# Local attention and a three-layer product: maxima one group ahead, a low part moved, one value product moved

## Chip, cores and metric

The kernel runs on one core of a Trainium2 chip. The metric is device time in microseconds of one execution, the median of the runs shown. TensorE (PE, with its weight loads as PEld), VectorE (DVE), ScalarE (ACT), GpSimd (POOL) and SyncE (SP) each work through a queue of their own, and wait for one another by semaphores.

## The reference

Four batches of eight heads, 768 positions, head size 64. A query sees the 96 keys up to itself and the first 8 keys, with a bias that falls with distance; after the softmax and the product with the values the heads are put together to 3072 rows of 512, which go through four matrices in fp32:

```python
scores = scale * np.matmul(q, k.transpose(0, 1, 3, 2)) + bias
scores = np.where(keep, scores, -1000000000.0)
a = np.exp(scores - np.max(scores, axis=-1, keepdims=True))
a = a / (np.sum(a, axis=-1, keepdims=True) + 1e-09)
x = np.matmul(a, v)            # then heads side by side: 3072 x 512
out = ((x @ w1) * (x @ w2)) @ w3 @ w_out
```

## The kernel before

**Attention.** Queries are cut into 24 blocks s of 128, and the blocks into 12 pairs d = s // 2. A block has four query groups q of 32. `scores` (line 684 on) makes all scores of a block on PE: for an even block the groups 0 and 1 go into two buffers of the shared PSUM pool (tile `more`), the rest into columns 104 to 511 of the tile `sc`. `maxima(s, q)` is two DVE instructions (line 709) that add the bias, take the row maximum and write the result to `pr`; `exponentials(s, q)` is two ACT instructions (line 716) on the same rows. `sums`, `scale_part` and `turn` (lines 721, 738, 746) are DVE's: reciprocal of the sums, scaling, and a transpose into `pt`. `values(d)` (line 760) multiplies a pair's transposed rows with the values on PE into columns 0 to 255 of `sc`, and `tokens(d)` (line 786) copies that on ACT into SBUF. So the scores of the next pair that lie in `sc` need that copy to be done.

**The products.** Two pairs make a unit of 512 rows. For unit 1 the first layer is done in 32 slices `U` of six 512-column matmuls (`first`, lines 278 to 280): per block f two slices, a gate copy on ACT (line 285), two slices, a product on DVE (line 288), a high part on ACT (line 293) and a low part on DVE (line 298). Beside that DVE and ACT build sums of weight blocks (`join`, `combine`, `sums_high`, `sums_low`, lines 200 to 213), which SP stores to DRAM and brings back (lines 218, 238). Units 2 to 5 do the same layer with seven half-size products (`Sevenths`, slices `P` of six 256-column matmuls, line 372), which gather in two PSUM tiles x and y and are taken out by ACT and DVE (lines 386 to 395); high and low part are lines 401 and 406. The last two products are folded into one: 32 slices `Z` of three 512-column matmuls (`third`, lines 310 to 312), eight for each of four row tiles t; the eighth of a tile needs the high and low part of the last block of the line. The tiles o, x, y, m and more share four PSUM buffers in turn.

**Order.** Up to unit 1 the order of all queues is written out by hand (`ORDER`). From there `planned` makes a list of slices, each with the work of ACT and DVE that follows it; entries marked 1 are issued after the matmuls of the next slice. `rounds(d, every, parts)` goes through a pair's two blocks and lets `on(k)` issue the next k slices in between; `go(place[...])` issues all slices up to a named one. On PE, ACT and DVE the instructions stand in the order written; SP's order is made by the framework's planner. A round of an odd pair begins with the last two `P` slices of its unit and goes on through `Z`; a round of an even pair from 6 on begins at slice 0 of tile t = 3 of the unit before, where `Z` and the first `P` slices of the next unit alternate, and where `first_tokens` and `next_tokens` (lines 81, 82, 795, 798) turn the copied tokens into high and low parts of the seven blocks.

Of the kernel before, what the change touches and what calls it, by code (L numbers as in the profile page):

```python
# [20 lines left out]
P = 128  # L21
# [10 lines left out]
NR = P // R  # L32
# [376 lines left out]
def line(u):  # L409

    return list(range(NFC)) if u % 2 == 0 or u < 2 else list(range(NFC))[::-1]
# [164 lines left out]
def banded(ctx, tc, ff, ns, nt, n1, nf, oki, qk, vx, sc, pr):  # L576
# [96 lines left out]
    def frame(s, q):  # L673

        return (0 if s % NB else WIN - R * q), KF

    def scored(s, u, q, w0, w1):

        if s < PAIRS:
            k = FR + q % 2 * KF  # L680
            return sc[:, 2 * u + q // 2, k + w0:k + w1]
        if s % 2 == 0 and q < 2:
            return more[s // 2][u][:, q * KF + w0:q * KF + w1]
        i, j = (q - 2, 0) if s % 2 == 0 else (q // 2, 1 + q % 2)
        k = F3 + j * KF
        return sc[:, 2 * u + i, k + w0:k + w1]
# [15 lines left out]
    def maxima(s, q):  # L702

        if q == 0:
            stats[s] = [at.tile([P, NR, 2], F32, tag=t, bufs=2, name=f"{t}_{s}") for t in ("mx", "sm")]
        w0, w1 = frame(s, q)
        for u in range(2):
            bias = (biasw if s % NB else bias0)[:, u, q, w0:w1]
            nc.vector.tensor_tensor_reduce(out=pr[:, q, u, GLB + w0:GLB + w1], in0=scored(s, u, q, w0, w1), in1=bias, scale=-SCALE, scalar=3.0e38, op0=ALU.add, op1=ALU.min, accum_out=stats[s][0][:, q, u:u + 1])  # L709
# [148 lines left out]
    def planned():  # L858

        def of(u, name):  # L860
            return lambda *x: getattr(units[u], name)(*x)

        last = NC // 2 - 1
        pieces = [(ff.sums_high, 2), (ff.sums_low, 2)]
        for k in range(3, NFC):
            pieces += [(ff.join, k), (ff.combine, k), (ff.sums_high, k), (ff.sums_low, k)]
        for f in range(NFC):
            for m in range(2):
                for half in range(2):
                    todo = [(0, of(1, "first"), f, m, half)]  # L870
                    if half:
                        todo += [(0, of(1, "gate"), f)] if m == 0 else [(0, of(1, "product"), f), (0, of(1, "high"), f), (1, of(1, "low"), f)]
                    elif f > 1:
                        todo += [(0, ff.blocks_out, f)] if m == 0 else []
                    if m == 0 or f > 3:
                        for _ in range(2 if m == half == 0 and f > 0 else 1):
                            if pieces and not (m and half):
                                call, k = pieces.pop(0)
                                todo.append((0, call, k))
                                if call == ff.sums_low:  # L880
                                    todo.append((0, ff.sums_out, k))
                    if (f, m, half) in ((5, 0, 0), (7, 1, 1)):
                        todo += [(0, ff.bring, k, g) for k in ((0, 2) if f == 5 else (1, 3)) for g in range(3)]
                    yield [("U", 1, f, m, half)] + todo
        assert not pieces

        def seventh(u, j, p):
            unit = of(u, "multiply"), of(u, "take")
            f = line(u)[j]
            todo = [(0, unit[0], p, f), (0 if p in (1, 5, 6, 7, 4) else 1, unit[1], p, f)]  # L890
            if p == 1 and j > 1:
                todo += [(0, of(u, "high"), line(u)[j - 2]), (1, of(u, "low"), line(u)[j - 2])]
            return [("P", u, j, p)] + todo

        for u in range(1, last + 1):
            if u > 1:
                for j in range(1, NFC):
                    for p in (1, 5, 4, 6, 2, 3, 7):
                        yield seventh(u, j - 1 if p in (4, 3) else j, p)
            tail = [seventh(u, NFC - 1, p) for p in (4, 3)] if u > 1 else []  # L900
            if tail:
                f = line(u)[-2]
                tail[0] += [(0, of(u, "high"), f), (1, of(u, "low"), f)]
            if u < last:
                yield from tail
                tail = []
            for t in range(2 * T // P):
                for j, f in enumerate(line(u)):
                    todo = [(0, of(u, "third"), t, f, line(u)[0], line(u)[-1])]
                    if j == NFC - 1:  # L910
                        todo.append((0, of(u, "store"), t))
                    if t == 0 and j == 3 and u > 1:
                        todo += [(0, of(u, "high"), line(u)[-1]), (0, of(u, "low"), line(u)[-1])]
                    if u < last and (t, j) == (1, 0):
                        todo.append((0, first_tokens, u + 1))
                    if u < last and (t, j) in ((2, 5), (2, 6), (3, 0), (3, 1), (3, 2), (3, 3)):
                        todo.append((0, next_tokens, u + 1))
                    yield [("Z", u, t, j)] + todo
                    if t == 0 and j in (1, 2) and tail:
                        yield tail.pop(0)  # L920
                    if t == 3 and j < 5 and u < last:
                        yield seventh(u + 1, 0, (1, 5, 6, 2, 7)[j])

    with tc.manual_schedule(engines={mybir.EngineType.PE}):
        with tc.manual_schedule(engines={mybir.EngineType.DVE, mybir.EngineType.SP, mybir.EngineType.Activation, mybir.EngineType.Pool}):
            ordered()
        with tc.manual_schedule(engines={mybir.EngineType.Activation, mybir.EngineType.DVE}):
            plan = list(planned())
            place = {x[0]: i for i, x in enumerate(plan)}
            done = [0]  # L930

            waiting = []

            def go(until):
                for _, *todo in plan[done[0]:until]:
                    (_, call, *x), *rest = todo
                    call(*x)
                    for call, x in waiting:
                        call(*x)
                    waiting.clear()  # L940
                    for late, call, *x in rest:
                        if late:
                            waiting.append((call, x))
                        else:
                            call(*x)
                done[0] = max(done[0], until)

            def on(k):
                go(done[0] + k)

            def rounds(d, every, parts):
                for s in (2 * d, 2 * d + 1):
                    for q in range(NR):
                        maxima(s, q)
                        exponentials(s, q)
                        on(every)
                    if parts > 1:
                        on(2)
                    sums(s)
                    cuts = [(k * NR // parts, (k + 1) * NR // parts) for k in range(parts)]  # L960
                    for step in (scale_part, turn):
                        for q0, q1 in cuts:
                            step(s, q0, q1)
                            if parts > 1:
                                on(1)
                    if parts == 1 and s % 2 == 0:
                        on(5)

            scores(STEPS)
            scores(STEPS + 1)  # L970
            for d in range(STEPS // 2, n // 2):
                u = d // 2 - 1
                load(d)
                ahead = [s for s in (2 * d + 2, 2 * d + 3) if s < n]
                for s in ahead:
                    keys(s)
                rounds(d, *((1, 1) if d % 2 else (1, 2) if u == 1 else (3, 2)))
                go(place["Z", u, 2, 5] if d % 2 else place["U", u, 5, 1, 0] if u == 1 else place["P", u, 5, 5])
                values(d)
                tokens(d)  # L980
                if ahead:
                    go(place["Z", u, 3, 0] if d % 2 else place["Z", u, 0, 0] if u == 1 else place["P", u, 7, 4])
                for s in ahead:
                    scores(s)
            ok = nc.values_load(oki[0:1, 0:1])
            tc.mark_branch_hint_location("rest", engines=(mybir.EngineType.SP, mybir.EngineType.Activation))
            go(len(plan))
# [40 lines left out]
```

## Time and profile before

| | |
|---|---|
| runs | 539.74, 538.71, 537.92 us; median 538.71 |
| profiled execution | 538.34 us, span 536.5 us |
| PE | 512.3 us busy (95%), 6148 matmuls |
| DVE | 355.1 us (66%) |
| ACT | 235.1 us (44%) |
| DMA | 107.32 MB, mean 200 GB/s |

PE is busy almost throughout; busy time of PE is modelled, so a stretch at half clock also counts as busy. DVE is above 90% up to some 190 us, where unit 1's first layer runs beside the weight sums, and near 60% after. The clock line of the page (tenths of full speed in 40 slices of 13.4 us) and the waits of single engines are in the rows below.

### The profile page before, as it was taken

Reading aid. Unit: us, or ns where it says so; the run is one execution under the profiler, and the core shown is the slowest. Engines: PE = TensorE matmul, PEld = TensorE weight load, DVE = VectorE, ACT = ScalarE, POOL = GpSimd, SP = SyncE. Lnnn points to the kernel's source line nnn. Section 1 sums busy time; section 2 is a strip of 40 time slices with the busy share of each in tenths; the row PEclk is TensorE's granted clock in tenths of the full one; section 3 lists DMA queues with packets and bytes.
Section 4 is the critical chain, followed back from the end, with each engine's and each line's share of the span. In section 5 each row is a group of like instructions: output and inputs, shape, how many; then the busy total and the mean of one; then the engine's idle time right before and its main releaser. Section 6 shows DMA issues by size and latency. Waiting matters only on the chain. (4 is left out here: it accounts for less than half of the span.)

```text
span 536.5 us, 14643 instructions
## 1 busy us (share of the span) xinstructions
PE 512.3 (95%) x6148; PEld 425.6 (79%) x6148; DVE 355.1 (66%) x914; ACT 235.1 (44%) x696; POOL 4.2 (1%) x29
## 2 busy tenths in 40 slices
PE   7899999999999899989998989998989998999997
PEld 5345468888888678879996879997879996899985
DVE  7899998985969876556656556556557456535520
ACT  2467766353542534555325355334455335423210
POOL 2000000000000000000000000000000000000000
PEclk9999999999999989999998999999999998999999
DMA  8996838983698979168713268703469500169001
GB/s 306 381 369 263 338 89 253 344 275 101 224 319 292 391 256 312 60 211 279 255 46 131 76 201 282 247 8 131 135 214 299 192 4 20 58 206 337 10 22 62
DMA packets 40155, 107.32 MB, mean 200 GB/s; under 512 B 3602, under 2 KB 22034, under 8 KB 38034
## 3 DMA queue, kind: packets, MB, share of 16 engines
q1 hardware_dynamic: 39936, 106.05, 56.8%
q8 instruction: 50, 0.82, 0.6%
q10 hardware_dynamic: 146, 0.26, 0.1%
q14 instruction: 23, 0.19, 0.1%
HBM read 83.23 MB, written 23.07 MB: 198 GB/s over the span
## 5 line engine op out<-in xcount | busy, mean ns | idle before, releaser
L716 ACT ACTIVATE pr<-pr,mx 128x136 f32<-128x136 f32 (+2 forms) x192 | 74.9, 391 | 71.9 <-DVE mx L709 71.3
L312 PE MATMUL o<-wh,gl 128*128 128x512 f32 x184 | 73.5, 399 | 5.2 <-DVE gl L406 5.2
L310 PE MATMUL o<-wh,gh 128*128 128x512 f32 x184 | 74.3, 404 | 0.2 <-issue 0.2
L311 PE MATMUL o<-wl,gh 128*128 128x512 f32 x184 | 73.3, 399 | 0.0
L386 ACT ACTIVATE ag<-x 128x256 f32<-128x256 f32 x64 | 24.5, 382 | 77.4 <-PE x L372 75.2
L372 PE MATMUL x<-xh,w12l 128*128 128x256 f32 x256 | 54.7, 285 | 0.0
L372 PE MATMUL x<-xh,w12h 128*128 128x256 f32 x256 | 54.4, 284 | 0.0
L278 PE MATMUL m<-xh,w12h 128*128 128x512 f32 x128 | 50.5, 394 | 0.0
L279 PE MATMUL m<-xl,w12h 128*128 128x512 f32 x128 | 49.9, 390 | 0.0
L280 PE MATMUL m<-xh,w12l 128*128 128x512 f32 x128 | 49.8, 389 | 0.0
L312 PEld LDWEIGHTS o<-wh,gl 128*128 128x128 f32 x184 | 35.4, 192 | 14.1 <-DVE gl L406 6.5
L372 PE MATMUL y<-xh,w12h 128*128 128x256 f32 x192 | 41.9, 288 | 3.9 <-DVE mx L709 3.8
L372 PEld LDWEIGHTS x<-xh,w12l 128*128 128x128 f32 x256 | 43.5, 191 | 0.9 <-issue 0.4
L372 PEld LDWEIGHTS x<-xh,w12h 128*128 128x128 f32 x256 | 43.4, 191 | 0.7 <-issue 0.2
L372 PE MATMUL y<-xh,w12l 128*128 128x256 f32 x192 | 41.8, 287 | 2.0 <-DVE mx L709 1.9
L310 PEld LDWEIGHTS o<-wh,gh 128*128 128x128 f32 x184 | 35.4, 192 | 7.8 <-issue 1.2
L311 PEld LDWEIGHTS o<-wl,gh 128*128 128x128 f32 x184 | 35.2, 191 | 6.2
L760 PEld LDWEIGHTS sc<-pt,vr 32*64 32x64 f32 x2112 | 31.8, 134 | 9.5 <-DVE pt L746 5.1
L760 PE MATMUL sc<-pt,vr 32*64 32x160 f32 (+4 forms) x2112 | 34.4, 272 | 3.9 <-DVE pt L746 3.8
L746 DVE STREAM_TRANSPOSE pt<-pr 128x1280 f32<-128x1280 f32 (+1 forms) x32 | 36.9, 1167 | 1.6 <-ACT pr L731 1.2
L406 DVE TENSOR_TENSOR gl<-ag,gh 128x512 fp32r<-128x512 f32 x32 | 21.9, 684 | 23.8 <-ACT gh L401 23.8
L372 PEld LDWEIGHTS y<-xh,w12h 128*128 128x128 f32 x192 | 32.6, 191 | 5.8 <-issue 4.6
(132 smaller groups left out, 990.0 us busy)
## 6 DMA issues: line engine op xcount, KB each, us to landing
qr<-qk SPq DMA_DIRECT2D x20, 720.0 KB, 6.6
w12h<-ws SPq DMA_DIRECT2D x20, 512.0 KB, 5.9
w12l<-ws SPq DMA_DIRECT2D x20, 512.0 KB, 5.5
w12h<-ws SPq DMA_DIRECT2D x10, 768.0 KB, 6.8
w12l<-ws SPq DMA_DIRECT2D x10, 768.0 KB, 6.8
vr<-vx SPq DMA_DIRECT2D x8, 768.0 KB, 4.4
out_dram<-ot SPq DMA_DIRECT2D x23, 256.0 KB, 2.6
raws<-w SPq DMA_DIRECT2D x5, 1024.0 KB, 6.3
```

Of the source, the lines that this page charges most:

```text
L278: self.nc.tensor.matmul(ps, lhsT=mh, rhs=xh[:, i], start=i == 0, stop=False)
L279: self.nc.tensor.matmul(ps, lhsT=mh, rhs=xl[:, i], start=False, stop=False)
L280: self.nc.tensor.matmul(ps, lhsT=ml, rhs=xh[:, i], start=False, stop=i == NCC - 1)
L310: self.nc.tensor.matmul(ps, lhsT=self.gh[:, f, ts], rhs=ff.wh[:, f], start=f == first, stop=False)
L311: self.nc.tensor.matmul(ps, lhsT=self.gh[:, f, ts], rhs=ff.wl[f], start=False, stop=False)
L312: self.nc.tensor.matmul(ps, lhsT=self.gl[:, f, ts], rhs=ff.wh[:, f], start=False, stop=f == last)
L372: self.nc.tensor.matmul(out, lhsT=w[:, i], rhs=x[:, i], start=p in (1, 5) and i == 0 and j == 0, stop=i == 1 and j == 2, skip_group_check= ...
L386: s.activation(e[(1, 6, 5).index(p)], y if p == 5 else x, AF.Copy)
L406: self.nc.vector.tensor_tensor(out=self.gl[:, f], in0=self.g[f], in1=self.gh[:, f].bitcast(F32), op=ALU.subtract)
L716: nc.scalar.activation(x, x, AF.Exp, bias=mx[:, q, u:u + 1], scale=-1.0, accum_out=sm[:, q, u:u + 1])
L746: nc.vector.transpose(strided(pts[d][:, (half * NR + q0) * 2 * PF:], [PF, 2 * (q1 - q0)], [P, NR + 1], [1, R]), x.rearrange("p n (k c) -> ...
L760: nc.tensor.matmul(sc[cols, hp, n0 * R:n1 * R], lhsT=v[rows, i, cols], rhs=turned, start=i == i0, stop=i == NV - 1, skip_group_check=True)
```

## The change

Three things are moved; no instruction is added or removed.

1. In `rounds`, the maxima of group q + 1 are issued ahead of the exponentials of group q, so that groups 0 and 1 stand together at a block's start.
2. In `planned`, for units 2 to 4 the high part of the line's last block is issued after `Z` slice 1 of tile 0 instead of slice 3, and its low part after the matmuls of slice 2. In odd rounds the sums of the even block come three slices later (the five slices that followed its transpose are split into three ahead of the sums and two behind the transpose). For unit 5 the high part stays and the low part comes one slice later.
3. `values(4)` and `tokens(4)` stand ahead of slice `U` 7.0.0 (number 28) instead of 5.1.0 (number 22): six slices later.

```diff
-                    if t == 0 and j == 3 and u > 1:
-                        todo += [(0, of(u, "high"), line(u)[-1]), (0, of(u, "low"), line(u)[-1])]
+                    if t == 0 and j == 1 and u > 1 and u < last or t == 0 and j == 3 and u == last:
+                        todo += [(0, of(u, "high"), line(u)[-1]), (1, of(u, "low"), line(u)[-1])]
...
             def rounds(d, every, parts):
                 for s in (2 * d, 2 * d + 1):
+                    maxima(s, 0)
                     for q in range(NR):
-                        maxima(s, q)
+                        if q < NR - 1:
+                            maxima(s, q + 1)
                         exponentials(s, q)
                         on(every)
-                    if parts > 1:
-                        on(2)
+                    on(2 if parts > 1 else 3 - s % 2 * 3)
                     sums(s)
...
                     if parts == 1 and s % 2 == 0:
-                        on(5)
+                        on(2)
...
                 rounds(d, *((1, 1) if d % 2 else (1, 2) if u == 1 else (3, 2)))
-                go(place["Z", u, 2, 5] if d % 2 else place["U", u, 5, 1, 0] if u == 1 else place["P", u, 5, 5])
+                go(place["Z", u, 2, 5] if d % 2 else place["U", u, 7, 0, 0] if u == 1 else place["P", u, 5, 5])
                 values(d)
                 tokens(d)
```

## Rows read from the trace of the kernel before

**Rows 1.** PE's waits from 130 us on: waiter, releaser, total us, times, longest.

```profile
PE y L372 <- DVE mx L709: 5.7, 3, 1.9
PE o L312 <- DVE gl L406: 5.2, 3, 1.8
PE sc L760 <- DVE pt L746: 3.8, 3, 2.5
```

**Rows 2.** The page: PE's granted clock in 40 slices, tenths of 2.4 GHz.

```profile
PEclk9999999999999989999998999999999998999999
```

**Rows 3.** Stretches: length, busy us (instructions) of each engine, granted clock, DMA.

```profile
189.70:193.10 3.40, 3.40 (x98) 3.24 (x99) 2.60 (x6) 0.63 (x1) 0.00 (x0) 0.50 0.96 326
292.10:295.50 3.40, 3.40 (x9) 2.64 (x8) 0.89 (x5) 2.75 (x10) 0.00 (x0) 0.50 0.20 77
...
296.00:299.40 3.40, 3.40 (x16) 2.81 (x15) 2.24 (x12) 1.91 (x9) 0.00 (x0) 1.00 0.02 5
```

**Rows 4.** Timeline, pair 6's start: start us, duration, engine, line, operation [idle before].

```profile
232.86 0.69 DVE L795 TENSOR_TENSOR xl<-more_raws,xh 128x512 fp32r<-128x512 f32 x1 [2.12 <-ACT xh L798]
...
234.07 0.22 DVE L709 CUSTOM_DVE_ANT_0 pr<-more,bias 128x72 f32<-128x72 f32 x1
...
234.45 0.35 PE L372 MATMUL y<-xh,w12h 128*128 128x256 f32 x1 [1.87 <-DVE mx L709]
```

**Rows 5.** Timeline of PE, pair 7: the low-part wait, and the values.

```profile
289.36 0.39 PE L311 MATMUL o<-wl,gh 128*128 128x512 f32 x1
291.55 0.50 PE L312 MATMUL o<-wh,gl 128*128 128x512 f32 x1 [1.80 <-DVE gl L406]
...
302.46 2.82 PE L760 MATMUL sc<-pt,vr 32*64 32x32 f32 x192
```

**Rows 6.** Timeline of DVE, pair 7: sums, low part, tokens, sums, transpose.

```profile
287.64 0.17 DVE L721 TENSOR_SCALAR sm<-sm 128x8 f32<-128x8 f32 x1 [0.74 <-ACT pr L716]
...
290.85 0.65 DVE L406 TENSOR_TENSOR gl<-ag,gh 128x512 fp32r<-128x512 f32 x1
...
294.89 1.22 DVE L82 TENSOR_TENSOR xl<-more_raws,xh 128x1024 fp32r<-128x1024 f32 x1 [2.51 <-ACT xh L81]
...
298.08 0.17 DVE L721 TENSOR_SCALAR sm<-sm 128x8 f32<-128x8 f32 x1 [1.09 <-ACT pr L716]
...
299.85 1.51 DVE L746 STREAM_TRANSPOSE pt<-pr 128x1280 f32<-128x1280 f32 x1
```

**Rows 7.** Timeline of ACT, pair 7: the last exponential of the odd block.

```profile
297.56 0.39 ACT L716 ACTIVATE pr<-pr,mx 128x136 f32<-128x136 f32 x1
```

**Rows 8.** Timeline of PE, pair 9: second part of the values.

```profile
380.63 2.12 PE L760 MATMUL sc<-pt,vr 32*64 32x160 f32 x128 [0.18 <-DVE pt L746]
```

**Rows 9.** Timeline of PE: the values of pair 4.

```profile
184.26 1.02 PE L760 MATMUL sc<-pt,vr 32*64 32x32 f32 x64
187.83 0.80 PE L760 MATMUL sc<-pt,vr 32*64 32x160 f32 x32 [2.54 <-DVE pt L746]
189.69 2.62 PE L760 MATMUL sc<-pt,vr 32*64 32x160 f32 x96 [1.06 <-DVE pt L746]
```

**Rows 10.** Timeline of DVE: products of blocks 4 and 6 of unit 1.

```profile
189.56 0.65 DVE L288 TENSOR_TENSOR ag<-m,ag 128x512 f32<-128x512 f32 x1
...
202.87 0.68 DVE L288 TENSOR_TENSOR ag<-m,ag 128x512 f32<-128x512 f32 x1
```

**Rows 11.** Timeline of ACT: pair 4's tokens, high part of block 6.

```profile
194.83 1.02 ACT L786 ACTIVATE more_raws<-sc 128x1024 f32<-128x1024 f32 x1
...
203.59 0.63 ACT L293 ACTIVATE gh<-ag 128x512 fp32r<-128x512 f32 x1 [1.41 <-DVE ag L288]
```

**Rows 12.** Timeline of PE: scores of pair 5, then the output product.

```profile
206.96 1.66 PE L700 MATMUL sc<-qr 64*32 64x136 f32 x96
208.55 0.50 PE L310 MATMUL o<-wh,gh 128*128 128x512 f32 x1
```

**Rows 13.** SP's queue: the load of pair 5's values.

```profile
198.22 0.40 SPq L670 DMA_DIRECT2D vr<-vx  x1
```

## The prediction

> **What bounds the kernel now.** Read the table of the page first: TensorE (PE) is busy 95% of the span, so only time in which it stands, or runs at half clock, can be won. The second view is the list of PE's waits from 130 us on, the stretch that the change touches [rows 1]. Three kinds hold nearly all of it: the second product of a seventh (tile y) behind maxima on VectorE (DVE), 5.7 us in three waits; the output product behind the low part gl, 5.2 us in three; the value product (tile sc) behind the transposes, 3.8 us in three. Third comes the granted clock: from 20 us on it is 2.4 GHz in all but three slices of the page [rows 2], each with one stretch at 1.2 GHz [rows 3]. A stretch of 3.4 us holds 16 of the 512-column matmuls at full clock (one every 0.227 us) and 9 at half: a fall takes (16 - 9) x 0.227 = 1.6 us. One fall is in the wait of pair 4's values, two follow the low-part waits of units 2 and 4 (the one from 449.1 on has the same row as that from 292.1); the third low-part wait and the three y waits have none. Last come timelines around each wait, for what would be late next.
>
> **Part 1: maxima one group ahead, even pairs 6, 8, 10 (three y waits).** [Rows 4], pair 6: y takes the PSUM buffer of the early scores, which is free when the maxima of group 1 have read it. DVE reaches them at 234.07, because they stand behind the residues of the next tokens, and those behind an ACT copy (DVE idle 2.12 us). In the new order they follow group 0 directly, near 230.1, inside that idle time, and cost it nothing (two instructions of some 0.2 us). PE's rows are 0.39 us long [rows 5] but follow each other every 0.23, so each idle of the list is 0.16 short of what the pace loses: 5.7 + 3 x 0.16 = 6.2 us. Next late is the low part of the third block: its residue (232.86 for 0.69) ends at 233.55, and the product that reads it would start at about 233.8, two slices after y; 0.2 us are left. I take 6.1; the bounds are 0 (another reader keeps the buffer) and 6.2. If the idle DVE time were gone, the 0.4 us of maxima would push that residue into PE's way by 0.3 a pair.
>
> **Part 2: low part ahead of the odd pair's sums (pairs 7, 9, 11).** [Rows 5, 6], pair 7: PE stops at 289.36 + 0.23 = 289.59 until 291.55, 1.96 us, for a low part (290.85) that stands behind sums, scaling and transpose (from 287.64 on). Issued after slice Z0.2 it goes into the 0.74 us that DVE idles before the sums: some 1.5 us before PE's need. So wait and fall both go, 1.96 + 1.6, and PE would reach this pair's values at 302.46 - 3.56 = 298.9. But then DVE's own chain to the odd block's transpose is late; it ended at 299.85 + 1.51 = 301.36. How much earlier it ends: sums to transpose start about 0.2 later than before (the low part waits for its high copy, and fills the idle), but 0.65 - 0.07 of low part is gone behind them: 0.37 earlier. In the odd block two maxima groups and four exponentials stood behind the first tokens' residue (294.89 to 296.11) and took until 298.08; with maxima one ahead it is one group and two exponentials, 0.39 us each [rows 7]: 0.8 less. Together 1.15 us, so 300.2. The value product needs the odd half after its first 64 of 192 matmuls (1.02 us with the last one's tail [rows 9], 0.8 to the next start): it waits at 299.7 for 0.5 us. Its second part began at 303.26 and begins at 300.25: 3.0 us won. Pair 11 repeats it with the same waits and fall: 3.0. Pair 9 had no fall and its values already waited for the transpose, until 380.63 [rows 8]: there only the 1.15 us of DVE's chain count. Sum 7.1 us; bounds 3.6 (the chain no earlier: 1.8 + 0 + 1.8) and 9.1 (no new wait: 5.7 + 3.2 of falls + 0.2).
>
> **Part 3: values of pair 4 six slices later.** Before, they start at 184.26, stand 2.54 and 1.06 us for the transposes and end at 189.69 + 2.62 = 192.31, with the clock falling [rows 3, 9]: 8.05 us for what takes 2.82 elsewhere [rows 5]; 0.5 more is lost to the rest of the fall. Moved, four slices (six matmuls, 1.365 us each) run from 184.26 to 189.7. The fifth takes the PSUM buffer of product 4, which DVE reads until 189.56 + 0.65 = 190.2 [rows 10]: 0.5 us. Two slices to 193.0, values without a wait to 195.85, four slices to 201.3. Now the next scores: their buffers are free when product 6 is through, 202.87 + 0.68 = 203.55, and nothing in DVE's chain from 189.56 to there waited for PE; it is residues, combinations and ACT copies. That is 2.2 us. The first 32 score matmuls run to 204.05. The other 96 write columns 104 to 511 of sc, of which the values hold 0 to 255 until the tokens' copy on ACT has read them. That copy was at 194.83 [rows 11]; in the new order it is issued behind the high part of block 6, which itself waits for product 6 (203.59): 204.12 to 205.14. Another 1.1 us, and the gate copy of block 7 behind it is 1 us later, without harm. Then 1.6 us of scores [rows 12], and the output product starts at 206.8 instead of 208.55: 1.75 us won, not the 5.7 that are lost now. PE stands some 3.3 us in two pieces there; that the clock falls again I put at one half, price 1.5: I take 1.0. Bounds: 0 and 5.2.
>
> SP's queue: the values' load for pair 5 waits for these values to be read. It was issued at 198.22 [rows 13]; the values now end at 195.85, so in the same place it waits for nothing. SP's order is not written by hand but planned; if the load were put ahead of the block-sum stores of 187 us, they would leave up to 8.8 us later and join 7 on DVE some 6 us later.
>
> **Edits at nothing.** Unit 5's low part one slice later: no attention work runs there, and four slices (2.7 us) cover its 0.65; without them, one wait of 2 us. Pair 5's sums three slices later: DVE has one low part between, so only names of slices change; its chain follows PE's 1 to 1.75. The five slices behind an even block become three and two: no instruction more. No DMA is added.
>
> Sum: 1.0 + 6.1 + 7.1 = 14.2 us. The profiled execution took 538.34 (span 536.5 and 1.8 around it), the median is 538.71: 524.1 against the first, 524.5 as the median.
>
> What the rows show of the clock is that two of six waits of about 2 us were followed by a fall. The Trainium skill (TensorE: Matmul & The Clock Gate, Part 1: The HAM clock gate) says that the moment of the decision does not follow the kernel's start, so that one kernel meets it elsewhere in another run; no run here shows that. By it the two falls of part 2 are a draw, and the median's gain would be one fall, 1.6 us, more or less.
>
> **Rivals.** (a) Part 3 in full: the scores wait for less than I think, no fall. For it: the slices themselves find all they need. Against: product 6 at 202.87. Gain up to 4.2 more: 520.3 to 523. (b) Odd values bound by DVE: its chain is not earlier, part 2 gives 3.6: 528.0. For it: pair 9 waited already; against: 0.8 us of exponentials do leave the chain. (c) The change doesn't do what it says: another reader holds y's buffer, part 1 gives 0: 530.6. Against: y starts at 234.45, just as these maxima end. (d) The planner moves pair 5's load forward: part 3 turns from +1.0 to about -4.6: 530.1. (e) Slower: the clock. With PE ahead of DVE, each stretch of values or scores (15 from 180 us on, all small matmuls) meets a short wait and a fall follows, 1.6 us each; from nine falls on the gain is gone, with 15 it is 24.0 against 14.2: 548.5. For it: the three falls stand beside waits. Against: the page shows no fall beside the other 14 of these stretches, and the waits I expect in them are 0.5 long.
>
> **How the numbers follow.** Forecast 0.55, (a) 0.13, (b) 0.18, (c) 0.06, (d) 0.05, (e) 0.03. The forecast's own spread is about 522 to 527. The range 520 to 530 takes in (a), (b) and the edge of (d) and leaves out (e), most of (c) and tails: under 0.15. Within 0.3% (1.6 us, about what a measurement of this kernel tells from no change) only a mixture of (c), (d) and falls can end: 0.02. Slower 0.03, faster 0.95.
>
> **What would show it.** Right: no wait of y for maxima; no wait of the output product for gl; pair 4's values in under 3 us, and PE standing at the scores after them, first for product 6, then for the tokens' copy; waits of half a microsecond in the values of pairs 7 and 11. Wrong: y waiting still, turns of pairs 7 to 11 ending as late against their scores as now, scores of pair 5 starting without a wait, or more than two stretches at 1.2 GHz.

## The result and the profile after

| | before | after |
|---|---|---|
| median of the runs, us | 539.23 (537.92 to 540.17, 4 runs) | 522.72 (522.31 to 523.54, 4 runs) |
| ratio, 95% interval | | 0.9697 [0.9672, 0.9723] |
| profiled execution, span | 538.34, 536.5 | 522.47, 520.6 |

The forecast was 524.5 with a range of 520 to 530. The total came out close. Of the three reasons for it one held, one held in sum with two errors that cancel, and one was wrong.

The list of PE's waits from 130 us on, which answers to [rows 1], shows it first. The waits of y and of the output product for gl are gone. The largest entry is new: 3.7 us in the value product, with "issue" in the place of a releaser, which means that PE waited for nothing that the profile shows.

```profile
PE sc L760 <- issue: 3.7, 1, 3.7
PE sc L760 <- DVE pt L746: 2.3, 3, 1.1
PE m L278 <- DVE ag L288: 0.3, 1, 0.3
```

The clock line of the page [rows 2] shows one slice below 9 behind the start-up in place of three:

```profile
PEclk9999999999999998999999999999999999999999
```

Two stretches (length, busy us with instructions of PE, PEld, DVE, ACT and POOL, granted clock, DMA share and GB/s) show what fills that slice [rows 3]: PE stands for 3.8 us, and then has 3.4 us at 1.2 GHz.

```profile
193.60:197.40 3.80, 0.14 (x11) 0.02 (x2) 3.07 (x6) 0.63 (x1) 0.00 (x0) 1.00 0.94 334
197.60:201.00 3.40, 3.40 (x31) 2.67 (x21) 2.19 (x4) 1.54 (x2) 0.00 (x0) 0.51 0.92 286
```

Pair 6, timelines of DVE and PE [rows 4]: the maxima of group 1 follow those of group 0 in the old idle time, and y starts without a wait.

```profile
228.52 0.22 DVE L709 CUSTOM_DVE_ANT_0 pr<-more,bias 128x72 f32<-128x72 f32 x1
...
230.91 0.28 PE L372 MATMUL y<-xh,w12h 128*128 128x256 f32 x1
```

Pair 7 [rows 5, 6]: on DVE the low part stands ahead of the sums. On PE the second part of the values waits for the odd block's transpose; the last line is the same wait in pair 9 [rows 8].

```profile
283.08 0.69 DVE L406 TENSOR_TENSOR gl<-ag,gh 128x512 fp32r<-128x512 f32 x1 [0.70 <-ACT gh L401]
283.69 0.17 DVE L721 TENSOR_SCALAR sm<-sm 128x8 f32<-128x8 f32 x1
...
292.88 0.17 DVE L721 TENSOR_SCALAR sm<-sm 128x8 f32<-128x8 f32 x1 [0.74 <-ACT pr L716]
294.65 1.51 DVE L746 STREAM_TRANSPOSE pt<-pr 128x1280 f32<-128x1280 f32 x1
```

```profile
294.60 1.02 PE L760 MATMUL sc<-pt,vr 32*64 32x32 f32 x64
296.22 2.12 PE L760 MATMUL sc<-pt,vr 32*64 32x160 f32 x128 [0.59 <-DVE pt L746]
...
370.00 2.12 PE L760 MATMUL sc<-pt,vr 32*64 32x160 f32 x128 [1.13 <-DVE pt L746]
```

The values of pair 4 on PE [rows 9] run without a wait for transposes, stand after 169 of their 192 matmuls, and the scores of pair 5 behind them wait for nothing [rows 12]:

```profile
191.13 2.61 PE L760 MATMUL sc<-pt,vr 32*64 32x32 f32 x169
197.40 0.49 PE L760 MATMUL sc<-pt,vr 32*64 32x64 f32 x23 [3.66 <-issue]
...
204.97 0.69 PE L700 MATMUL more<-qr 64*32 64x136 f32 x32
205.46 1.66 PE L700 MATMUL sc<-qr 64*32 64x136 f32 x96
207.05 0.50 PE L310 MATMUL o<-wh,gh 128*128 128x512 f32 x1
```

**Where the time came from.** The span cut at the starts of PE's stages gives this table, in us. A stretch runs from its first matmul's start to the first matmul's start behind it; that of an odd pair begins at the first matmul behind its scores. The columns of the experiments are told of further down.

| stretch | before | after | maxima only | low part only | values only |
|---|---|---|---|---|---|
| start to unit 1's first layer | 154.11 | 152.27 | 153.03 | 153.33 | 153.07 |
| unit 1 first layer to its output product | 54.44 | 54.79 | 54.56 | 54.43 | 55.03 |
| even pairs 6, 8, 10: first slices to values | 33.23, 33.30, 33.32 | 30.66, 30.64, 30.64 | 30.63, 30.66, 30.65 | 33.22, 33.27, 33.28 | 33.22, 33.31, 33.29 |
| odd pairs 7, 9, 11: behind the scores to behind the values | 22.47, 20.63, 22.78 | 19.59, 19.59, 19.90 | 19.61, 19.06, 19.92 | 22.89, 21.30, 21.69 | 20.87, 20.63, 22.74 |

Even pairs give 7.9 us, odd pairs 6.8, unit 1 loses 0.35: 14.4 us by the change, against 14.2 in the sum. The two profiled spans differ by 15.9: unit 1 starts 1.8 earlier, and the stretches that the table leaves out are together 0.3 longer. Ahead of unit 1 the three edits change nothing, and in the twelve later profiles with the same instructions there, its start lies between 152.27 and 153.95. So it varies between runs of one order, and no edit is credited with it.

### The profile page after: what moved, and what is told of

Its sections match the earlier page's. It is cut to its first block, busy times and chain, and to the rows that moved or that the text cites. A ratio compares the mean times of both kernels' runs of the same rounds, so it can differ in the third digit from the quotient of the medians.

```text
span 520.6 us, 14640 instructions
## 1 busy us (share of the span) xinstructions
PE 506.7 (97%) x6148; PEld 423.6 (81%) x6148; DVE 354.8 (68%) x914; ACT 233.1 (45%) x696; POOL 4.2 (1%) x29
## 5 line engine op out<-in xcount | busy, mean ns | idle before, releaser
L310 PE MATMUL o<-wh,gh 128*128 128x512 f32 x184 | 73.0, 397 | 0.2 <-issue 0.2
L311 PE MATMUL o<-wl,gh 128*128 128x512 f32 x184 | 71.9, 391 | 0.0
L312 PE MATMUL o<-wh,gl 128*128 128x512 f32 x184 | 71.7, 390 | 0.0
L372 PE MATMUL x<-xl,w12l 128*128 128x256 f32 x128 | 36.2, 283 | 0.0
```

The costliest lines, as they stand in the source:

```text
L310: self.nc.tensor.matmul(ps, lhsT=self.gh[:, f, ts], rhs=ff.wh[:, f], start=f == first, stop=False)
L311: self.nc.tensor.matmul(ps, lhsT=self.gh[:, f, ts], rhs=ff.wl[f], start=False, stop=False)
L312: self.nc.tensor.matmul(ps, lhsT=self.gl[:, f, ts], rhs=ff.wh[:, f], start=False, stop=f == last)
L372: self.nc.tensor.matmul(out, lhsT=w[:, i], rhs=x[:, i], start=p in (1, 5) and i == 0 and j == 0, stop=i == 1 and j == 2, skip_group_check= ...
```

## The experiments

Each was timed beside the kernel before on the same chip (median 539.17 us in the first four, 537.13 in the next four, 538.17 in the next three, 539.16 in the last). Three of them turned out to have the order of another kernel on every engine, and serve as repeats: "later weights" of the changed kernel (523.76 against 522.72), "all three" and "without low part" of "values earlier" (516.46 and 515.89 against 516.06). So about 1 us is what two times of one order may differ by. Their ratios to the kernel before differ by up to 0.5% (0.9748 and 0.9697), since that kernel's median moves by 2 us from chip to chip; small differences are therefore read from the stretches of the traces, which repeat within 0.1 us where the orders are the same and no wait or clock fall differs.

**1. Maxima only.** Part 1 alone; the low part, the slices ahead of the sums and the place of the values are those of before.

```diff
+                    maxima(s, 0)
                     for q in range(NR):
-                        maxima(s, q)
+                        if q < NR - 1:
+                            maxima(s, q + 1)
```

> The kernel before with the maxima one group ahead and nothing else. Theory A (the parts share one DVE chain): besides the three y waits (7.9 us in the changed kernel with the short P waits behind them) the early maxima let the sums of the odd pairs' even block start some 1.1 us earlier, so the low part behind them is only 0.8 us late instead of 1.96, and the odd transpose ends 1.9 us earlier. Low-part waits of about 0.8 us each remain, the two stretches at 1.2 GHz go: 15 us less than before, 524 (527 if the falls stay). Rival B (the parts add up as the prediction has them): only the y part, 6 to 8 us, 531 to 533, with low-part waits of 1.8 to 2.0 us as before.

Measured: 523.01 us (521.21 to 524.2), ratio 0.9707 [0.9679, 0.9734], the time of the whole change. The even pairs are those of after, and so, within 0.6 us, are the odd pairs. Its waits from 130 us on:

```profile
PE sc L760 <- DVE pt L746: 2.5, 2, 2.0
PE o L312 <- DVE gl L406: 1.8, 3, 0.6
```

The low-part waits remain, at 0.6 in place of 1.8, and no fall of the clock follows them. Pair 7's values don't wait. So PE loses some 0.8 us at the low part (0.6 and 0.16 of pace), where the changed kernel loses 0.83 in the values. The odd block's transpose now ends 1.0 us before the second part of the values starts:

```profile
294.26 1.51 DVE L746 STREAM_TRANSPOSE pt<-pr 128x1280 f32<-128x1280 f32 x1
```

**2. Low part only.** Part 2 alone; the slices around the odd rounds' sums are those of the change too.

```diff
-                    if t == 0 and j == 3 and u > 1:
-                        todo += [(0, of(u, "high"), line(u)[-1]), (0, of(u, "low"), line(u)[-1])]
+                    if t == 0 and j == 1 and u > 1 and u < last or t == 0 and j == 3 and u == last:
+                        todo += [(0, of(u, "high"), line(u)[-1]), (1, of(u, "low"), line(u)[-1])]
```

> The kernel before with the low part of the last block ahead of the odd pair's sums (and the three and two slices) and nothing else. Theory A: without early maxima the high part on ACT still follows four late exponentials, so the sums come 0.5 us later than before; the low-part waits and their falls go, but the values of pairs 7, 9 and 11 then wait for the transposes 2 to 3 us: 2 us less than before in all, 537. Rival B: 7 us less, 532, with waits of 0.5 us in the values of pairs 7 and 11.

Measured: 541.97 us (538.64 to 543.46), ratio 1.006 [1.0035, 1.0084]: a little slower than before. The low-part waits are gone, but not the time; the values wait for the transposes instead, and the clock falls behind that wait in pair 7 (128 matmuls take 3.63 us, against 2.12 in the changed kernel).

```profile
PE sc L760 <- DVE pt L746: 11.0, 5, 2.8
PE y L372 <- DVE mx L709: 5.7, 3, 1.9
...
299.92 1.51 DVE L746 STREAM_TRANSPOSE pt<-pr 128x1280 f32<-128x1280 f32 x1
301.49 3.63 PE L760 MATMUL sc<-pt,vr 32*64 32x160 f32 x128 [2.31 <-DVE pt L746]
```

The table's stretches sum to no change (odd pairs +0.42, +0.67, -1.09), where theory A had expected 2 us less. The profiled execution was its fastest, with a mean granted clock of 0.990; the other six have 0.981 to 0.984, so they spend more time at 1.2 GHz. Where these falls lie, the one trace doesn't tell.

**3. Values only.** Part 3 alone: the line with `place["U", u, 7, 0, 0]`.

> The kernel before with pair 4's values six slices later and nothing else. Theory T1 (PE runs out of instructions inside these values): from the start of unit 1's first layer to its output product 54.4 us before becomes 54 to 55, a stand of 3 to 4 us without a releaser after some 169 of 192 value matmuls, one stretch at 1.2 GHz after it; the whole within 0.3% of before. The forecast's part 3: 1.75 us less, no stand inside the values, the stand at the scores instead.

Measured: 537.31 us (534.94 to 539.11), ratio 0.9977 [0.9951, 1.0003]. The stand is there by itself, at the same matmul, and unit 1's stretch is 0.6 longer than before:

```profile
192.16 2.61 PE L760 MATMUL sc<-pt,vr 32*64 32x32 f32 x169
198.48 0.65 PE L760 MATMUL sc<-pt,vr 32*64 32x64 f32 x23 [3.71 <-issue]
```

**4. Phase.** The changed kernel with 50 more matmuls, and so 100 more instructions on PE, in the warm-up at the start.

> The changed kernel with 50 more dummy matmuls at the very start (42 to 92), where PE waits for its first transfers anyway: 100 instructions more ahead of everything. Theory T1: PE's instructions come in blocks of 256 that are fetched when a block is used up; the shift puts the block boundary elsewhere, so pair 4's values run through in about 2.8 us, and what my part 3 expected shows instead: a stand at pair 5's scores until product 6 and the tokens' copy are done; the output product starts 2 us earlier after the start of the layer (52.5 instead of 54.8). Instead short stands of up to 1 us without a releaser may show inside the values of pairs 8 and 10, where the new boundaries fall. Rival T2 (a wait that the profile doesn't show, tied to the data of these values): the stand stays after about 169 of 192 matmuls, 3 to 4 us, and nothing appears in pairs 8 and 10.

Measured: 526.91 us (525.63 to 529.61), ratio 0.9789 [0.9757, 0.9821]. The values of pair 4 run through, and behind them stand the waits that the forecast had put there, for product 6 and for the tokens' copy; unit 1's stretch is 53.08. The clock falls there too (0.50 from 205.0 to 208.4), as the prediction had put at one half. The stand has gone elsewhere: in the values of pair 8 it comes after 167 of 192, and in those of pair 10, 1.56 us long, after 159. These two and a later start of unit 1 (153.87) make most of the 3.8 us by which the profiled span is longer than the changed kernel's, though unit 1's stretch is 1.7 shorter.

```profile
192.48 2.82 PE L760 MATMUL sc<-pt,vr 32*64 32x32 f32 x192
202.88 0.69 PE L700 MATMUL more<-qr 64*32 64x136 f32 x30 [0.96 <-DVE ag L288]
204.45 2.57 PE L700 MATMUL sc<-qr 64*32 64x136 f32 x96 [0.88 <-ACT more_raws L786]
...
333.46 2.58 PE L760 MATMUL sc<-pt,vr 32*64 32x32 f32 x167
337.16 0.44 PE L760 MATMUL sc<-pt,vr 32*64 32x64 f32 x25 [1.11 <-issue]
```

So the stand belongs to the number of the instruction, not to data: PE had no instructions left. The other traces say the same. In all ten that have part 3's stand and no extra instructions (the changed kernel and experiments 3 and 5 to 12) it comes ahead of the same matmul, the 2134th of the trace, whether that lies in the values or, with the values issued earlier, in the first layer's products behind them.

**5. Tokens late.** The changed kernel with `first_tokens` five slices later.

```diff
-                    if u < last and (t, j) == (1, 0):
+                    if u < last and (t, j) == (1, 5):
                         todo.append((0, first_tokens, u + 1))
```

> The changed kernel, with the first tokens' residue issued five key slices later in the output product's stretch, so that DVE takes both groups of maxima and ACT their exponentials of the odd block first. Theory S (the waits that are left in the values of pairs 7, 9 and 11, 0.83, 1.37 and 0.83 us, end with a chain on DVE and ACT that this residue lengthens): the three waits go, the odd stretches (scores to the end of the values, 19.59, 19.59 and 19.90 us) come to about 18.8, the total to 519.7 (3.0 less than 522.7). Rival (the residue is wanted soon, and DVE has no idle time left for it later): the values no longer wait, but the next first-layer or attention step does, and the total stays at 522 to 523.5.

Measured: 520.04 us (519.71 to 520.69), ratio 0.9676 [0.9652, 0.9699]. The odd stretches are 18.68, 18.20 and 18.98, 3.2 us less than after, and no wait for `pt` is left from 130 us on. DVE takes the sums of pair 7's odd block, and its transpose, ahead of the tokens' residue, which the changed kernel has between them and the even block:

```profile
293.62 1.51 DVE L746 STREAM_TRANSPOSE pt<-pr 128x1280 f32<-128x1280 f32 x1
295.05 1.18 DVE L82 TENSOR_TENSOR xl<-more_raws,xh 128x1024 fp32r<-128x1024 f32 x1
```

**6. Later weights.** Loads of the next unit's weights put later in the plan.

```diff
-                    if (f, m, half) in ((5, 0, 0), (7, 1, 1)):
-                        todo += [(0, ff.bring, k, g) for k in ((0, 2) if f == 5 else (1, 3)) for g in range(3)]
+                    if (f, m, half) == (7, 1, 1):
+                        todo += [(0, ff.bring, k, g) for k in (0, 2, 1, 3) for g in range(3)]
```

> The changed kernel, with all twelve loads of the next unit's weights issued at the later of their two places, so that fewer DMAs are under way while pair 4's values run. Theory T1a (PE stands 3.7 us inside the values of pair 4 because the packet with its next 256 instructions waits behind the weights on the DMA engines): the stand shrinks to 1 to 1.5 us, the stretch from unit 1's first layer to its output product from 54.79 to about 52.5, total 520.3. Rival T1b (the delay of a packet is the same whatever else is on the DMA engines): the stand stays at 3.5 us or more and the total at 522.7. If the weights then come too late, PE waits for them at the next unit's start, from about 228 us on, and the total is above 523.

Measured: 523.76 us (522.32 to 525.48), ratio 0.9748 [0.9719, 0.9776], with a stand of 3.77 us after 169. It tells nothing on the question: the planner left SP's order as it was, and the DMA engines were as full as in the changed kernel (share 0.92 during the stand).

**7. Values earlier.** Later tokens, and pair 4's values at slice 24.

```diff
-                go(place["Z", u, 2, 5] if d % 2 else place["U", u, 7, 0, 0] if u == 1 else place["P", u, 5, 5])
+                go(place["Z", u, 2, 5] if d % 2 else place["U", u, 6, 0, 0] if u == 1 else place["P", u, 5, 5])
```

> The changed kernel with the later tokens' residue of the run before, and with the values of pair 4 moved two slices later than before the change in place of six (slice 24 for 28), so that they end ahead of the place at which PE's instructions ran out or straddle it by little. Theory T1 (the stand belongs to the instruction's number and to the time of its packet): it comes 2 to 4 us after the values or at their end, 2.7 to 4.8 us in all with what is left of the transposes' wait, the scores of pair 5 wait for product 6 alone; unit 1's stretch 52.6 to 54.6, total 518 to 519.6. Rival (the stand belongs to the values): it stays inside them at 3.7 us beside the transposes' wait of 1 to 2 us, and the total is that of the later residue alone, 519.7 or more.

Measured: 516.06 us (515.35 to 516.71), ratio 0.9599 [0.9575, 0.9623], an interval below that of the changed kernel. Unit 1's stretch is 51.06, 1.5 better than the low end of what was expected: the stand falls behind the values and is 0.47 long, since the packet with the next instructions came 1.1 us after its call (how the call is estimated stands further down) and the transposes' wait of 0.65 gave it time. No slice of the clock line is below 9.

```profile
187.89 1.57 PE L760 MATMUL sc<-pt,vr 32*64 32x160 f32 x96 [0.65 <-DVE pt L746]
...
190.36 0.40 PE L279 MATMUL m<-xl,w12h 128*128 128x512 f32 x1 [0.47 <-issue]
```

**8. All three.** Edits 5, 6 and 7 together.

> The three edits together: later tokens' residue, later weights, values of pair 4 two slices later than before the change. If the three gains add: unit 1's stretch 51.4 to 52.5 (from 51.4 on product 6 on DVE bounds it), odd stretches 18.8 each, total 516 to 517. If the weights' place does nothing (T1b), the time of the run before, 518 to 519.6. If late weights hold up the next unit, above that run by 0.5 or more.

Measured: 516.46 us (515.11 to 517.28), ratio 0.9606 [0.958, 0.9631]. As the weights' edit moves nothing, it repeats 7.

**9. Small loads.** The DMA traffic itself is taken away: the kernel leaves out seven eighths of every load of these weights (112 of 128 partitions).

```diff
-        self.nc.sync.dma_start(out=self.slot(f)[:, k0 - 1:k1 - 1].bitcast(F32), in_=self.ws[f, :, k0:k1])
+        self.nc.sync.dma_start(out=self.slot(f)[:16, k0 - 1:k1 - 1].bitcast(F32), in_=self.ws[f, :16, k0:k1])
```

> The changed kernel, in which every load of the second and later units' weights (w12h, w12l) brings 16 of its 128 partitions and leaves the others as they were, so that about half of the bytes under way on the DMA engines from 180 to 197 us are gone, with PE's instructions the same. (The run before that moved these loads in the plan left them where they were in SP's queue, so it told nothing.) Theory T1a (the stand of PE inside the values of pair 4 is a packet of instructions held up by other DMAs): the packet comes within 2 us of its call, about 193 us at the latest in place of 195.15, the stand of 3.7 us shrinks to 0.5 to 2, the scores of pair 5 wait for product 6 instead, unit 1's stretch 52.5 to 53.5 (from 54.79), total 520.5 to 521.5. Rival T1b (a packet needs that long whatever else the DMA engines do): the stand stays at 3.5 us or more, stretch 54.8, total 522.7.

Measured: 520.38 us (519.75 to 521.35), ratio 0.9671 [0.9645, 0.9697], unit 1's stretch 52.17. The stand is at the same matmul and 2.3 us shorter; ahead of it the DMA share is 0.10, where the changed kernel has 0.76 (191.13 to 193.60) and 0.94.

```profile
191.71 2.61 PE L760 MATMUL sc<-pt,vr 32*64 32x32 f32 x169
195.66 0.43 PE L760 MATMUL sc<-pt,vr 32*64 32x64 f32 x23 [1.35 <-issue]
...
190.00:193.10 3.10, 3.10 (x110) 2.52 (x116) 1.82 (x6) 1.21 (x2) 0.00 (x0) 1.00 0.10 32
```

So these loads hold the packet up (T1a), for most of the stand; 1.35 us of it are left without them. The busy share of the DMA engines as such does not: between the call and the packet's start it is 1.00 to 1.04 in experiments 7, 8, 10, 11 and 12, where the traffic is stores of the weight sums and some smaller loads, and the packet starts 1.1 to 1.8 us after its call. The trace of the changed kernel points at one load, of 768 KB:

```profile
191.01 0.32 SPq L238 DMA_DIRECT2D w12h<-ws  x1
```

Its 128 packets of 6 KB start from 191.97 to 195.03, and the instruction packet follows at 195.15. In experiments 3, 5 and 6 the instruction packet (195.91 to 196.19) likewise starts among the last packets of this load. That it is this load and no other is read from these times and was not tested by itself; in the kernel before the packet came 3.0 us after its call with 512-KB loads and stores under way, so it can be delayed without it.

**10. One slice more.** Kernel 7 with the values at slice 25.

> The fastest kernel so far (later tokens' residue, values of pair 4 at slice 24) with these values one slice later, at 25. Theory T1 (PE's instructions come in blocks of 256, and the block's end is met at a fixed instruction): each slice is 12 instructions, in the changed kernel (slice 28) the end came after 169 of the 192 value matmuls, so here it comes after 187 of them, at 189.1 us, and the stand is 1.5 to 2.1 us if the packet needs as long as at slice 24; no wait for the transposes; total within 0.8 of 516.1. Rival (the stand is set by DVE or by data): no stand after 187 matmuls, the values run through or wait for the transposes as before.

Measured: 517.27 us (515.78 to 518.99), ratio 0.9609 [0.9581, 0.9636]. The place and length are as theory T1 had them:

```profile
188.17 2.77 PE L760 MATMUL sc<-pt,vr 32*64 32x32 f32 x187
192.50 0.31 PE L760 MATMUL sc<-pt,vr 32*64 32x32 f32 x5 [1.56 <-issue]
...
192.90:196.10 3.20, 3.20 (x8) 2.51 (x9) 2.28 (x3) 1.37 (x2) 0.00 (x0) 0.50 0.15 48
```

The total missed its bound (1.2 above kernel 7). In the profiled execution, the slowest of the six (518.99), a clock fall follows the stand, unit 1's stretch is 52.21, and PE stands once more, for 1.32 us, in the values of pair 6. Runs of it with a mean clock of 0.999 and above took 515.78 and 517.68.

**11. Without low part.** Meant to undo part 2 in kernel 7, it put back only the slice of the low part.

> The fastest kernel so far (maxima ahead, later tokens' residue, values of pair 4 at slice 24) with the last block's low part put back behind the odd pair's sums, so that part 2 of the change is undone in it alone. Theory A2 (part 2 pays only when the chain to the odd block's transposes is shorter, as here): three waits of the output product for gl of 0.8 us come back, no clock falls, odd stretches 0.7 to 0.9 longer each, total 518.2 to 518.9. Rival B2 (the falls belong to these waits): with two falls of 1.6 us beside them 521.5. Rival C2 (the waits move into the values and the low part's place is worth nothing): 516 to 516.5.

Measured: 515.89 us (514.92 to 518.17), ratio 0.9591 [0.9562, 0.962]. The order on DVE hangs on the slices ahead of the sums and did not change; it repeats 7.

**12. Part two undone.** Kernel 7 with the slices ahead of the sums put back as well.

```diff
-                    on(2 if parts > 1 else 3 - s % 2 * 3)
+                    if parts > 1:
+                        on(2)
...
                     if parts == 1 and s % 2 == 0:
-                        on(2)
+                        on(5)
```

> The fastest kernel (maxima ahead, later tokens' residue, values of pair 4 at slice 24) with the whole of part 2 undone: the low part's slice and also the slices ahead of the sums, on which the order on DVE hangs. (The run before put back the low part's slice alone; in its trace the low part still stood ahead of the sums, so it was the fastest kernel once more and told nothing of part 2.) Theory A2 (part 2 pays once the chain to the odd block's transposes no longer bounds the values): three waits of the output product for gl of 0.7 to 0.8 us come back, without clock falls, odd stretches 0.7 to 0.9 longer each, total 518.2 to 518.9 against 516. Rival B2 (the clock falls behind these waits come back): two falls of 1.6 us beside them, 521.5. Rival C2 (the low part's place is worth nothing): 515.9 to 516.5.

Measured: 518.55 us (517.28 to 521.08), ratio 0.9626 [0.9597, 0.9654]. Odd stretches are 19.60, 19.07 and 19.96, 2.8 us more than in 7; three waits for gl are back and no clock fall:

```profile
PE o L312 <- DVE gl L406: 1.8, 3, 0.6
PE sc L760 <- DVE pt L746: 0.7, 1, 0.7
```

## Why the prediction was right or wrong

**Part 1** (6.1 us for the even pairs): the mechanism was right, the size too small. The even stretches give 7.9. Pair 6's first slices to y took 4.23 us and take 2.22, so 2.01 is the y wait, as worked out (1.87 + 0.16). Another 0.56 a pair lies behind y, in steps between 256-column matmuls that were 0.20 to 0.31 us long instead of 0.12. Most of these go, presumably since DVE's chain is some 2 us earlier; no run separates that. The list of waits does not name them, and the step "each idle of the list is 0.16 short" left them out. The feared push on the next residue did not come.

**Part 2** (7.1 us for the odd pairs): the size was right to 0.3 us (2.88, 1.04 and 2.88 measured, 3.0, 1.15 and 3.0 forecast), and the forecast waits in the values of pairs 7 and 11 are there, 0.59 and 0.60 long. But the credit was wrong, and the sum came out right because two errors cancel. By experiments 1 and 2 part 1 alone gives 7.3 here and part 2 alone nothing. The end of the odd block's transposes, counted from the first score matmul of its pair (pairs 7, 9, 11, in us), shows what each part does to DVE's chain:

| | before | maxima only | low part only | after |
|---|---|---|---|---|
| start of the even block's sums | 6.97, 6.53, 6.97 | 5.74, 5.43, 5.74 | 8.10, 7.66, 8.10 | 7.09, 6.80, 7.10 |
| end of the odd block's transposes | 20.69, 20.37, 20.68 | 18.67, 18.42, 18.67 | 21.36, 21.03, 21.36 | 19.57, 19.33, 19.57 |

The prediction had 1.15 us earlier in all, and 1.04 to 1.12 is measured. But it made this of 0.8 from the maxima and 0.37 from the low part. The maxima give 2.0: the 0.8 in the odd block were worked out, the 1.2 that they give the even block's sums were left out. The low part gives not 0.37 earlier but 0.7 to 0.9 later. The step that failed there is "sums to transpose start about 0.2 later than before": they start 1.1 to 1.4 later. The low part does not fit into DVE's idle 0.74 us before the sums, because its high copy stands behind the exponentials on ACT; in the kernel before it ends at 288.12, when the sums (287.64) have begun:

```profile
287.51 0.61 ACT L401 ACTIVATE gh<-ag 128x512 fp32r<-128x512 f32 x1
```

The other step that failed is "So wait and fall both go", booked as the low part's own gain. With the maxima alone the low part is no more than 0.8 us late, and no fall follows; with both, that 0.8 is lost in the values instead, where PE now waits for DVE's later chain. Only when the chain is shortened elsewhere, so that the transposes no longer end late (tokens' residue, experiment 5), is part 2 worth anything: 518.55 - 516.06 = 2.5 us (experiment 12), and 2.8 in the odd stretches.

**Part 3** (1.0 us): wrong in sign and in mechanism. Unit 1's stretch is 0.35 longer (54.43 to 54.56 in the three traces with the values at slice 22, 54.69 to 55.10 in the four with them at slice 28, full loads and no extra instructions). The step that failed is "values without a wait to 195.85": data were ready, as forecast, but instructions were not. The waits forecast for the scores were sound, and experiment 4 shows both; in the changed kernel DVE and ACT catch up while PE stands, so the scores start at 204.97 without a wait. The clock fall to which the prediction gave one half came, behind the stand. Of the signs that the prediction named for being wrong, one is there: scores of pair 5 that start without a wait. Of those for being right, one is missing: values of pair 4 in under 3 us. DVE is also less full up to unit 1's end than the section on the time before has it: 113.1 us of the first 130 and 58.4 of the next 70, so 87% and 83%.

Why PE ran out of instructions: the page counts 50 packets on an instruction queue, 0.82 MB in all, for 6148 matmuls and as many weight loads.

```profile
q8 instruction: 50, 0.82, 0.7%
```

That is 16.4 KB and some 246 instructions each. The Trainium skill (Runtime: NRT & Kernel Launch, Instruction fetch mechanics) says that blocks of 256 instructions are fetched while the current one runs and that the cost of a boundary is mostly hidden. The traces agree with the first: 16.4 KB a packet, and a stand tied to the number of the instruction. With 18 matmuls and 18 weight loads fewer ahead of the values (three slices, experiment 10 against the changed kernel) it moves from after 169 to after 187 of them. They disagree with the second for this stage. Taking 256 for a block, and a packet called when one block is used up and one is left, the call comes 128 matmuls ahead of the stand, by estimate at 191.59 in the changed kernel. Its packet starts in the trace at 195.15, 3.6 us later, and PE goes on at 197.40, another 2.25. In "small loads" the packet starts 1.0 after the call and PE goes on 2.5 later; in "one slice more" 1.4 and 2.3. The 128 matmuls take only 128 x 2.82 / 192 = 1.9 us in the values. So the stand is the packet's delay, plus 2.3 to 2.5, less 1.9 and the last matmul's 0.2. That the next packet is called with one block left is an assumption that fits these times; no run tests it by itself. Before, the same count puts the call at 188.05, the packet started at 191.02, 3.0 later, and PE came to the same matmul only at 195.7, 13 matmuls behind the values: the waits for transposes [rows 9] and the clock fall in between hid the delay.

**Rivals.** (a) comes near by its total alone: the scores start without a wait, but after a stand and a fall. (b) is what happened where part 2 stands alone, and worse: DVE's chain is not only no earlier but 0.7 later, and part 2 gives 0 and not 3.6. (c) and (d) did not occur: y no longer waits, and the load of pair 5's values was issued at 203.62, behind the values as before [rows 13]. (e) did not occur; one fall is left where three were. That falls differ between runs of one order shows in "values only": pair 7's low-part wait is 1.80 us there too, and its odd stretch is 20.87 instead of 22.47, one fall of 1.6 less. The rule that the prediction took from the Trainium skill (TensorE: Matmul & The Clock Gate, Part 1: The HAM clock gate), that one kernel meets the decision elsewhere in another run, agrees with that row. It agrees too with the kernel before itself: in its runs beside the experiments the mean granted clock lies between 0.976 and 0.992 (median 0.986), where the profiled execution with its three falls has 0.990.

That the total of 14.4 comes so near to 14.2 is luck: the sum is 1.8 too small in part 1 against 1.35 too large in part 3 and 0.3 in part 2, and part 2 hides two errors of its own. The medians differ by 16.5, with the 1.8 ahead of unit 1 that no edit made. So the total does not show that the three terms were understood.

## What to carry to other kernels

When two edits bear on the same late engine, follow the end of its chain for each edit alone, and not only the waits. Before moving an instruction into an engine's idle time, look whether its own input is there by then: here the low part's was not, and it pushed back all that stood behind it. A sum that comes out right may hold two errors. A stretch of very short matmuls that waits for data may be covering a wait for instructions; before taking the data wait away, find the instruction packets in the trace, see which large loads are issued just ahead of them, and compare their delay with the time that the instructions in hand will last.

## What the runs showed of the hardware that was not expected

- PE can run out of instructions. With 192 matmuls and 192 weight loads in 2.82 us, it stood 3.66 to 3.78 us in the four traces where a 768-KB load of weights was under way, 1.35 us with seven eighths of that load gone, and 0.3 to 1.6 us at other places. The profile names such a wait "issue", at an instruction in the middle of a run of the same form.
- An instruction packet's delay does not follow the busy share of the DMA engines: by the estimate of its call it was 1.1 to 1.8 us at a share of 1.00 to 1.04 without the 768-KB load (3.0 in the kernel before), and 3.6 us at 0.87 to 0.92 with it.
- The waits of 0.6 us for gl were followed by no fall in "maxima only" and "part two undone"; those of 1.8 us were followed by one in some traces and not in others (pair 7 before, but not in "values only"). The clock fell behind all stands of 3.66 us and more, and behind one of 1.56 us in "one slice more", but not behind one of 1.56 us in "phase".
